# First MLP's second product on token blocks of 384 instead of 288

## The chip, the core and the metric

The kernel runs on one core of a Trainium2 chip. The metric is device time of one execution in microseconds (us). Before the change it is 1552.22 us, the median of three runs (1552.0 to 1557.69).

## What is computed

Two-step attention through 32 packed vectors per head, then two MLPs, all in float32 (8 batches, 8 heads, 576 tokens, so 4608 tokens of 512 features):

```python
p_packed = sm_attn(p, k, v)
out = sm_attn(q, p_packed, p_packed)
x = out.transpose(0, 2, 1, 3).reshape(4608, 512)
a = x @ w_a
b = x @ w_b
y = a * b @ w_out
h = y @ w_in
g = h * np.clip(h + 3.0, 0.0, 6.0) / 6.0
result = g @ w_out2
```

The change concerns `a * b @ w_out`, with d_ff = 1536.

## The kernel before, in words

A float32 product is made of three TensorE matmuls on values that are split into a high and a low part (`mm3`, lines 58 to 61: hi·hi on L59, lo·hi on L60, hi·lo on L61). Names ending in `_hi` and `_lo` are these parts.

**First stage.** Attention and the first MLP are interleaved. The outer loop has 48 steps `t`: four groups `g` of two batches (1152 tokens), and in each twelve blocks `m` of 128 hidden features. A step issues five units, in this order: `ab_unit(t, 0, 0)`, `pw_unit(t + 1)`, `ab_unit(t, 0, 1)`, `ab_unit(t, 1, 0)`, `ab_unit(t, 1, 1)`.

- `pw_unit` (L409 to L415) multiplies packed vectors and first-layer weights for the next step into two PSUM banks of the kind `att` (three exist); ScalarE makes `pw_hi` (L411), VectorE `pw_lo` (L415), which frees the banks.
- `ab_unit(t, b, h)` computes a and b of the hidden block for one half (288 tokens, `SH`) of one batch: 12 matmuls, 6 into each of two PSUM tiles, out of three `ab` banks. ScalarE copies a out (L435), VectorE multiplies by b (L437, `g`). Two ticks later `rest` makes `g_hi` on ScalarE (L443) and `g_lo` on GpSimd (L444). A tick is one unit or one `y_unit`.
- `y_unit(g, s, oc, r)` is the second product: for one block of 128 output features (`oc`, four of them), one token block `r` and three steps t (`SW` = 3), 9 matmuls into one of two `y` banks. The sum over the four `s` of a group is kept in SBUF (`acc`): copied by ScalarE for s = 0 (L462), added by VectorE after (L464), and stored to `y1d` at s = 3 (L466). Before, r counts four token blocks of 288, the same blocks that `ab_unit` makes.

So each three steps make 16 y units. They wait in a list, `y_ready`, and are put out one at a time at chosen places between the five units of a step. A y unit issued beside an `ab_unit` is what TensorE does while ScalarE and VectorE empty the `ab` banks.

Beside this, ScalarE, VectorE and GpSimd convert the weights from float64 (`piece_units`: `cv_` tiles and L81 to L96, results `rab`, `ro`, `p2f`), split `w_out` (`wo_split`, L392 and L393) and do the attention's softmax for the next batches (`s`, `et`, `pv`, `bd` are its products on TensorE). In most steps of the first group three pieces are converted (`w_a`, `w_b`, `w_out`), in the second and third group one piece for the second MLP, and two in every third step (t = 14, 17, up to 35). Each engine takes its instructions in the order in which the program issues them; the table of places in the step loop sets this order.

**Second stage.** The second MLP runs on tiles of 768 tokens, with products `h` (384 columns) and `o` (512 columns). The change does not touch it.

Of the kernel before, what the change touches and what calls it, by code (L numbers as in the profile page):

```python
# [8 lines left out]
F32 = mybir.dt.float32  # L9
F32R = mybir.dt.float32r  # L10
# [9 lines left out]
B, H, S, D, NP = 8, 8, 576, 64, 32  # L20
NT = B * S
DM, F1, F2 = 512, 1536, 2048
P = 128
NM1 = F1 // P
NM2 = F2 // P
SH = S // 2
NG = B // 2
TG = 2 * S
SW = 3
# [3 lines left out]
CP = 512  # L33
# [7 lines left out]
def f32(ap):  # L41
    return ap.bitcast(F32)
# [3 lines left out]
def tile_kernel(ctx: ExitStack, tc: tile.TileContext, qT, kT, vn, pT, wab, wo1, win, wo2, out):  # L46
# [9 lines left out]
    act, dve, pool, pe, sp = nc.scalar, nc.vector, nc.gpsimd, nc.tensor, nc.sync  # L56
# [46 lines left out]
    p2f = dram.tile([NM2, 2, P, CP], F32, name="p2f")  # L103
    y1d = dram.tile([DM // P, P, NT], F32, name="y1d")
# [7 lines left out]
    main = es_main.enter_context(tc.tile_pool(name="main", bufs=1))  # L112
    psum = es_main.enter_context(tc.tile_pool(name="psum", bufs=1, space=PSUM))
# [6 lines left out]
    def later(n, fn):  # L120
        due.append([n, fn])
# [232 lines left out]
    def piece_units():  # L354
        k = n_piece[1]
        n_piece[1] += 1
        m, i = pieces[k]
        if m >= NM1:
            o = att.tile([P, CP], F32, tag="p2f", name=f"p2f{m}_{i}", bufs=3)
            stores.append((p2f[m - NM1, i], o))  # L360
        elif i == 2:
            o = ro_tile(m)
            stores.append((wo1f[m * P:(m + 1) * P, :], o))
        else:
            if i == 0:
                rab_tile(m)
            o = rab_t[m][:, i * CP:(i + 1) * CP]
            stores.append((wabf[m][:, i * CP:(i + 1) * CP], o))

        def move():  # L370
            if k > 0 and k != n_first:
                sp.dma_start(*stores[k - 1])

        u = f64_round(att, raw64.pop(k), o, f"p{m}_{i}")
        last = u.pop()

        def end():
# [44 lines left out]
    def ab_unit(t, b, h):  # L422
        hi, lo = pw_t[t]
        ath, atl = at_t[2 * (t // NM1) + b]
        r = 2 * b + h
        ps = []
        for w in range(2):
            pt = psum.tile([P, 512], F32, tag="ab", name=f"ab{t}_{r}{w}", bufs=BANKS["ab"])[:, :SH]
            for c in range(2):
                ws = slice(w * P, (w + 1) * P)  # L430
                ts = slice(h * SH, (h + 1) * SH)
                mm3(pt, hi[:, c, b, ws], lo[:, c, b, ws], ath[:, c, ts], atl[:, c, ts], c == 0, c == 1)
            ps.append(pt)
        a = main.tile([P, SH], F32, tag="a", name=f"a{t}_{r}", bufs=2)
        act.copy(a, ps[0])  # L435
        g32 = main.tile([P, SH], F32, tag="g32", name=f"g32_{t}_{r}", bufs=3)
        dve.tensor_mul(g32, a, ps[1])  # L437
        gh = main.tile([P, SH], F32R, tag=f"g_hi{r}", name=f"g_hi{t}_{r}", bufs=SW + 1)
        gl = main.tile([P, SH], F32R, tag=f"g_lo{r}", name=f"g_lo{t}_{r}", bufs=SW + 1)
        g_t[t, r] = (gh, gl)  # L440

        def rest():
            act.copy(gh, g32)  # L443
            pool.tensor_sub(gl, g32, f32(gh))  # L444
            if t % SW == SW - 1:
                later(2, lambda: y_ready.extend((t // NM1, t % NM1 // SW, oc, r) for oc in range(DM // P)))

        later(2, rest)

    y_ready = []  # L450

    def y_unit(g, s, oc, r):
        ps = psum.tile([P, 512], F32, tag="y", name=f"y{g}_{s}{oc}{r}", bufs=BANKS["y"])[:, :SH]
        for i in range(SW):
            t = g * NM1 + s * SW + i
            gh, gl = g_t[t, r]
            oh, ol = wo_t[t, oc // 2]
            ws = slice(oc % 2 * P, (oc % 2 + 1) * P)
            mm3(ps, oh[:, ws], ol[:, ws], gh, gl, i == 0, i == SW - 1)
        if s == 0:  # L460
            acc_t[oc, r] = main.tile([P, SH], F32, tag=f"acc{oc}{r}", name=f"acc{g}_{oc}{r}", bufs=1)
            act.copy(acc_t[oc, r], ps)  # L462
        else:
            dve.tensor_add(acc_t[oc, r], ps, acc_t[oc, r])  # L464
        if s == NM1 // SW - 1:
            sp.dma_start(y1d[oc, :, g * TG + r * SH:g * TG + (r + 1) * SH], acc_t[oc, r])  # L466

# [212 lines left out]
    for t in range(NSTEP):  # L680
        g, m = divmod(t, NM1)
        if m == 0 and g + 1 < NG:
            lhs_tiles(g + 1)
            b = 2 * g + 2
# [28 lines left out]
        for i, (u, *x) in enumerate(units):  # L713
# [17 lines left out]
            for k in range(2):  # L731
                for _ in parts[2 * i + k]:
                    if not now:
                        now = piece_units()
                    now.pop(0)()
                for fn in todo[2 * i + k]:
                    fn()
                if y_ready and (k == 0 or i in (1, 3)) and (y_ready[0][0] * NM1 + y_ready[0][1] * SW + SW - 1, y_ready[0][2] // 2) in wo_t:
                    y_unit(*y_ready.pop(0))
                    tick()  # L740
    while due or y_ready:
# [193 lines left out]
```

## Time and profile before

| | us |
|---|---|
| median of three runs | 1552.22 |
| lowest, highest | 1552.0, 1557.69 |
| profiled execution, its own time | 1552.25 |
| profiled execution, its span | 1550.5 |
| TensorE matmul busy | 1491.7 (96% of the span) |
| weight loads busy | 1347.3 (87%) |
| VectorE busy | 872.3 (56%) |
| ScalarE busy | 682.0 (44%) |
| GpSimd busy | 491.9 (32%) |

A matmul's row shows a duration that reaches past the start of the next matmul, since they are pipelined; the distance between starts is the pace. Idle time in brackets at a row's end is that of the engine just before it, with what ended it. About 1.75 us of the execution lie outside the span.

### The profile page before, as it was taken

To read this page: it belongs to the slowest core of one execution; us is meant where nothing else is said; L and a number is where in the kernel's file an instruction comes from. 1 tells how busy PE (TensorE), PEld (TensorE's weight loads), DVE (VectorE), ACT (ScalarE), POOL (GpSimd) and SP (SyncE) were. 2 spreads that over 40 slices of the span, in tenths; PEclk is the share of its full clock that TensorE was granted. 3 is DMA by queue.
4 is the path that set the end of the run, shared out by engine and by line. 5 is a ranking of instruction groups with operands and counts; after the bars stand their busy time and mean duration, and the time that the engine had idled before them with its cause. 6 is when DMAs were issued, how large, how long until landed. Compare 5 with 4: busy or idle time off the path is not lost. (4 is left out here: it accounts for less than half of the span.)

```text
span 1550.5 us, 27991 instructions
## 1 busy us (share of the span) xinstructions
PE 1491.7 (96%) x11128; PEld 1347.3 (87%) x11128; DVE 872.3 (56%) x1592; ACT 682.0 (44%) x1453; POOL 491.9 (32%) x483
## 2 busy tenths in 40 slices
PE   4799999999999999999999999999999999999998
PEld 2588898888989899999989988998998998998997
DVE  5778784555754666545544464455455446455443
ACT  4566554554555545554423343343343334234332
POOL 2576653453634545554711130030020021011000
PEclk9799999999999999999999999999999999999999
DMA  8775555655466433664354334344344344333331
GB/s 288 218 220 177 184 191 176 194 160 179 124 198 188 138 125 106 235 219 170 120 180 178 129 141 178 116 162 149 130 152 167 107 172 143 136 144 133 142 138 41
DMA packets 75954, 250.06 MB, mean 161 GB/s; under 512 B 7856, under 2 KB 26288, under 8 KB 68784
## 3 DMA queue, kind: packets, MB, share of 16 engines
q1 hardware_dynamic: 75824, 248.28, 46.6%
q8 instruction: 87, 1.43, 0.4%
q14 instruction: 43, 0.35, 0.1%
HBM read 196.87 MB, written 51.38 MB: 160 GB/s over the span
## 5 line engine op out<-in xcount | busy, mean ns | idle before, releaser
L59 PE MATMUL ab<-at_hi,pw_hi 128*128 128x288 f32 x768 | 234.0, 305 | 8.3 <-ACT a L435 5.5
L61 PE MATMUL ab<-at_hi,pw_lo 128*128 128x288 f32 x768 | 229.1, 298 | 4.3 <-DVE pw_lo L415 4.3
L59 PE MATMUL y<-g_hi,wo_hi 128*128 128x288 f32 x768 | 231.3, 301 | 1.8 <-DVE acc L464 1.7
L60 PE MATMUL ab<-at_lo,pw_hi 128*128 128x288 f32 x768 | 228.6, 298 | 1.2 <-POOL at_lo L291 0.6
L61 PE MATMUL y<-g_hi,wo_lo 128*128 128x288 f32 x768 | 226.4, 295 | 1.0 <-POOL wo_lo L393 1.0
L60 PE MATMUL y<-g_lo,wo_hi 128*128 128x288 f32 x768 | 226.9, 295 | 0.4 <-POOL g_lo L444 0.4
L60 PE MATMUL o<-wo_lo,g2h 128*128 128x512 f32 x576 | 225.0, 391 | 0.0
L61 PE MATMUL o<-wo_hi,g2l 128*128 128x512 f32 x576 | 224.9, 390 | 0.0
L59 PE MATMUL o<-wo_hi,g2h 128*128 128x512 f32 x576 | 224.7, 390 | 0.0
L444 POOL TENSOR_TENSOR g_lo<-g,g_hi 128x288 fp32r<-128x288 f32 x192 | 164.4, 859 | 176.8 <-ACT g_hi L443 172.4
L783 DVE TENSOR_TENSOR g2l<-u,g2h 128x384 fp32r<-128x384 f32 x192 | 121.7, 634 | 140.9 <-ACT g2h L782 136.0
L437 DVE TENSOR_TENSOR g<-a,ab 128x288 f32<-128x288 f32 x192 | 86.4, 451 | 171.7 <-PE ab L61 112.3
L59 PEld LDWEIGHTS ab<-at_hi,pw_hi 128*128 128x128 f32 x768 | 146.6, 191 | 23.7 <-ACT a L435 7.6
L59 PEld LDWEIGHTS y<-g_hi,wo_hi 128*128 128x128 f32 x768 | 144.2, 188 | 19.4 <-DVE acc L464 9.1
L774 ACT ACTIVATE r<-c,half_b 128x384 f32<-128x384 f32 x144 | 88.9, 617 | 144.4 <-DVE c L767 143.9
L61 PEld LDWEIGHTS ab<-at_hi,pw_lo 128*128 128x128 f32 x768 | 146.3, 191 | 4.6 <-DVE pw_lo L415 4.5
L60 PEld LDWEIGHTS ab<-at_lo,pw_hi 128*128 128x128 f32 x768 | 146.5, 191 | 1.7 <-POOL at_lo L291 0.9
L570 POOL TENSOR_TENSOR ty_T<-raw_y 128x768 f32<-128x768 f32 x12 | 23.4, 1952 | 387.1 <-DMA raw_y<-y1d 387.1
L435 ACT COPY a<-ab 128x288 f32<-128x288 f32 x192 | 76.2, 400 | 157.9 <-PE ab L61 156.9
L61 PEld LDWEIGHTS y<-g_hi,wo_lo 128*128 128x128 f32 x768 | 144.3, 188 | 1.5 <-POOL wo_lo L393 1.5
L60 PEld LDWEIGHTS y<-g_lo,wo_hi 128*128 128x128 f32 x768 | 144.3, 188 | 0.6 <-POOL g_lo L444 0.6
L782 ACT CAST g2h<-u 128x384 fp32r<-128x384 f32 x192 | 98.7, 514 | 86.1 <-DVE u L776 84.7
(323 smaller groups left out, 3058.1 us busy)
## 6 DMA issues: line engine op xcount, KB each, us to landing
w<-w2d SPq DMA_DIRECT2D x47, 1792.0 KB, 7.3
rab<-wabf SPq DMA_DIRECT2D x36, 512.0 KB, 5.2
f64p<-in_wo SPq DMA_DIRECT2D x28, 512.0 KB, 3.7
w2d<-w SPq DMA_DIRECT2D x8, 1792.0 KB, 6.7
f64p<-in_wab SPq DMA_DIRECT2D x24, 512.0 KB, 4.6
k<-in_kT SPq DMA_DIRECT2D x16, 576.0 KB, 5.3
q<-in_qT SPq DMA_DIRECT2D x16, 576.0 KB, 5.2
ro<-wo1f SPq DMA_DIRECT2D x36, 256.0 KB, 3.7
```

Source lines behind the costliest of these rows:

```text
L59: pe.matmul(ps, lhsT=l_hi, rhs=r_hi, start=first, stop=False, skip_group_check=skip)
L60: pe.matmul(ps, lhsT=l_hi, rhs=r_lo, start=False, stop=False, skip_group_check=skip)
L61: pe.matmul(ps, lhsT=l_lo, rhs=r_hi, start=False, stop=last, skip_group_check=skip)
L435: act.copy(a, ps[0])
L437: dve.tensor_mul(g32, a, ps[1])
L444: pool.tensor_sub(gl, g32, f32(gh))
L570: pool.tensor_sub(z[to], get(a), get(b))
L774: act.activation(r, c, AF.Relu, bias=half_b, scale=1.0 / 6.0)
L782: act.copy(hi, u)
L783: dve.tensor_sub(lo, u, f32(hi))
```

## The change

The first product keeps its units of 288 tokens. The gated product of one batch is now one tile of 576 (`g32`), whose halves ScalarE and VectorE fill in place (the separate tile `a` is gone). When the second half is there, it is split into hi and lo parts by pieces that belong to three token blocks of 384 per group: 384 + 192 tokens of the first batch, 192 + 384 of the second (`PLACE`). The second product has three blocks r of 384, so 12 y units in three steps instead of 16. It is put out in at most five places of a step (before: seven). One conversion buffer (`p2f`) is given up: two in place of three.

```diff
+TY = 384
+
+PLACE = {0: [(0, TY, 0, 0), (TY, S, 1, 0)], 1: [(0, S - TY, 1, S - TY), (S - TY, S, 2, 0)]}
...
-            o = att.tile([P, CP], F32, tag="p2f", name=f"p2f{m}_{i}", bufs=3)
+            o = att.tile([P, CP], F32, tag="p2f", name=f"p2f{m}_{i}", bufs=2)
...
-        a = main.tile([P, SH], F32, tag="a", name=f"a{t}_{r}", bufs=2)
-        act.copy(a, ps[0])
-        g32 = main.tile([P, SH], F32, tag="g32", name=f"g32_{t}_{r}", bufs=3)
-        dve.tensor_mul(g32, a, ps[1])
-        gh = main.tile([P, SH], F32R, tag=f"g_hi{r}", name=f"g_hi{t}_{r}", bufs=SW + 1)
-        gl = main.tile([P, SH], F32R, tag=f"g_lo{r}", name=f"g_lo{t}_{r}", bufs=SW + 1)
-        g_t[t, r] = (gh, gl)
-
-        def rest():
-            act.copy(gh, g32)
-            pool.tensor_sub(gl, g32, f32(gh))
-            if t % SW == SW - 1:
+        if h == 0:
+            g32_t[0] = main.tile([P, S], F32, tag="g32", name=f"g32_{t}_{b}", bufs=3)
+        g32 = g32_t[0]
+        part = g32[:, h * SH:(h + 1) * SH]
+        act.copy(part, ps[0])
+        dve.tensor_mul(part, part, ps[1])
+        if h == 0:
+            return
+
+        def rest(t0, t1, r, r0):
+            n = t1 - t0
...
+            gh, gl = (x[:, r0:r0 + n] for x in g_t[t, r])
+            act.copy(gh, g32[:, t0:t1])
+            pool.tensor_sub(gl, g32[:, t0:t1], f32(gh))
+            if t % SW == SW - 1 and r0 + n == TY:
                 later(2, lambda: y_ready.extend((t // NM1, t % NM1 // SW, oc, r) for oc in range(DM // P)))
 
-        later(2, rest)
+        for i, x in enumerate(PLACE[b]):
+            later(2 + i, lambda x=x: rest(*x))
...
-        ps = psum.tile([P, 512], F32, tag="y", name=f"y{g}_{s}{oc}{r}", bufs=BANKS["y"])[:, :SH]
+        ps = psum.tile([P, 512], F32, tag="y", name=f"y{g}_{s}{oc}{r}", bufs=BANKS["y"])[:, :TY]
...
-                if y_ready and (k == 0 or i in (1, 3)) and (y_ready[0][0] * NM1 + y_ready[0][1] * SW + SW - 1, y_ready[0][2] // 2) in wo_t:
+                if y_ready and k == 0 and (y_ready[0][0] * NM1 + y_ready[0][1] * SW + SW - 1, y_ready[0][2] // 2) in wo_t:
```

How the order moves, in the step t = 14 (a third step of its three). First TensorE, before. `ab_10`, `ab_11` are the two PSUM tiles of `ab_unit(14, 0, 1)`, `ab_20` and `ab_30` those of the second batch's halves, the digits of `y_012` are s, oc and r. Of each unit the first row is shown:

```order
L59 MATMUL ab_30_3757<-at_hi_3231,pw_hi_3342 128x288
...
L59 MATMUL ab_00_3840<-at_hi_1739,pw_hi_3599 128x288
...
L409 MATMUL pw_0_3875<-rab_3364,lhs_697 32x256
...
L59 MATMUL ab_10_3915<-at_hi_1739,pw_hi_3599 128x288
...
L59 MATMUL ab_20_3945<-at_hi_3231,pw_hi_3599 128x288
...
L59 MATMUL y_000_3969<-g_hi_0_3318,wo_hi_3366 128x288
...
L59 MATMUL y_010_3983<-g_hi_0_3318,wo_hi_3366 128x288
...
L59 MATMUL ab_30_3995<-at_hi_3231,pw_hi_3599 128x288
...
L176 MATMUL s_400_4015<-q_3340,lhs_3297 32x288
...
L59 MATMUL y_020_4029<-g_hi_0_3318,wo_hi_3431 128x288
...
L176 MATMUL s_410_4043<-q_3340,lhs_3297 32x288
```

The same place now:

```order
L63 MATMUL ab_30_3425<-at_hi_2997,pw_hi_3069 128x288
...
L63 MATMUL y_312_3458<-g_hi_2_2689,wo_hi_2609 128x384
...
L63 MATMUL ab_00_3518<-at_hi_1648,pw_hi_3294 128x288
...
L63 MATMUL y_322_3545<-g_hi_2_2689,wo_hi_2650 128x384
...
L413 MATMUL pw_0_3564<-rab_3091,lhs_686 32x256
...
L63 MATMUL y_332_3594<-g_hi_2_2689,wo_hi_2650 128x384
...
L63 MATMUL ab_10_3616<-at_hi_1648,pw_hi_3294 128x288
...
L63 MATMUL ab_20_3640<-at_hi_2997,pw_hi_3294 128x288
...
L63 MATMUL ab_30_3663<-at_hi_2997,pw_hi_3294 128x288
...
L180 MATMUL s_400_3683<-q_3067,lhs_3023 32x288
...
L180 MATMUL s_410_3697<-q_3067,lhs_3023 32x288
...
L63 MATMUL ab_00_3711<-at_hi_1648,pw_hi_3562 128x288
```

Every y unit now has an `ab_unit` or the `pw_unit` on either side; in place of `ab_30`, `ab_00`, `pw`, `ab_10`, `ab_20` in a row, now the four units `ab_10`, `ab_20`, `ab_30`, `ab_00` follow each other without a y unit, which makes three bare successions in every three steps; and the attention's `s_400` and `s_410` have no y unit between them.

ScalarE in the same step, before:

```order
L411 CAST pw_hi_3873<-pw_0_3875 128x512
L411 CAST pw_hi_3873<-pw_1_3876 128x512
L443 CAST g_hi_0_3858<-g_14_0_3856 128x288
L392 CAST wo_hi_3899<-ro_3555 128x256
L81 ACTIVATE cv_sqp_1_3908<-f64p_1_3176 128x512
L82 ACTIVATE p2f_1_3907<-f64p_1_3176 128x512
L435 COPY a_1_3929<-ab_10_3915 128x288
L435 COPY a_2_3959<-ab_20_3945 128x288
L443 CAST g_hi_1_3933<-g_14_1_3931 128x288
```

And now:

```order
L415 CAST pw_hi_3562<-pw_0_3564 128x512
L415 CAST pw_hi_3562<-pw_1_3565 128x512
L396 CAST wo_hi_3586<-ro_3251 128x256
L85 ACTIVATE cv_sqp_1_3609<-f64p_1_2936 128x512
L86 ACTIVATE p2f_1_3608<-f64p_1_2936 128x512
L442 COPY g_14_0_3532<-ab_10_3616 128x288
L442 COPY g_14_1_3654<-ab_20_3640 128x288
L455 CAST g_hi_0_3657<-g_14_0_3532 128x384
L442 COPY g_14_1_3654<-ab_30_3663 128x288
```

One `g_hi` has left the stretch between `pw_hi` and the copy out of `ab_10`.

VectorE in the same step, before:

```order
L84 TENSOR_SCALAR cv_ap_1_3911<-f64p_1_3176 128x512
L437 TENSOR_TENSOR g_14_1_3931<-a_1_3929,ab_11_3922 128x288
L415 TENSOR_TENSOR pw_lo_3874<-pw_0_3875,pw_hi_3873 128x512
L415 TENSOR_TENSOR pw_lo_3874<-pw_1_3876,pw_hi_3873 128x512
L88 SCALAR_TENSOR_TENSOR cv_ap_1_3911<-f64p_1_3176,cv_ap_1_3911 128x512
```

And now:

```order
L477 TENSOR_TENSOR acc_32_1638<-y_332_3594,acc_32_1638 128x384
L419 TENSOR_TENSOR pw_lo_3563<-pw_0_3564,pw_hi_3562 128x512
L419 TENSOR_TENSOR pw_lo_3563<-pw_1_3565,pw_hi_3562 128x512
L88 TENSOR_SCALAR cv_ap_1_3612<-f64p_1_2936 128x512
L443 TENSOR_TENSOR g_14_0_3532<-g_14_0_3532,ab_11_3623 128x288
L92 SCALAR_TENSOR_TENSOR cv_ap_1_3612<-f64p_1_2936,cv_ap_1_3612 128x512
```

`pw_lo` now stands ahead of the multiplication that needs `ab_11`, and behind the addition that needs the y unit after `pw`.

## Rows read from the trace of the kernel before

**Rows 1.** Busy time of each engine in three stretches: start, both stages.

```profile
core 0: us, PE busy (x) PEld busy (x) DVE busy (x) ACT busy (x) POOL busy (x), PEclk, DMA share, GB/s
0.00:100.00 100.00, 66.83 (x828) 48.16 (x829) 69.22 (x133) 53.55 (x122) 46.40 (x46) 0.86 0.78 252
100.00:794.00 694.00, 678.86 (x6566) 627.00 (x6565) 420.08 (x799) 352.17 (x830) 358.07 (x387) 1.00 0.52 169
794.00:1550.00 756.00, 745.99 (x3739) 672.11 (x3737) 382.97 (x662) 276.31 (x501) 87.47 (x51) 1.00 0.39 143
```

**Rows 2.** TensorE's waits from 100 to 790 us: total, times, longest.

```profile
PE s L176 <- DVE pw_lo L415: 4.7, 4, 2.7
PE ab L59 <- ACT a L435: 4.2, 7, 0.7
PE pw L409 <- POOL rab L96: 2.3, 2, 1.8
PE y L59 <- DVE acc L464: 1.7, 2, 1.3
...
PE y L60 <- POOL g_lo L444: 0.4, 1, 0.4
...
PE y L61 <- POOL wo_lo L393: 0.3, 1, 0.3
```

**Rows 3.** Costliest groups of the page: the second product's matmuls.

```profile
L59 PE MATMUL y<-g_hi,wo_hi 128*128 128x288 f32 x768 | 231.3, 301 | 1.8 <-DVE acc L464 1.7
L61 PE MATMUL y<-g_hi,wo_lo 128*128 128x288 f32 x768 | 226.4, 295 | 1.0 <-POOL wo_lo L393 1.0
L60 PE MATMUL y<-g_lo,wo_hi 128*128 128x288 f32 x768 | 226.9, 295 | 0.4 <-POOL g_lo L444 0.4
```

**Rows 4.** Timeline of TensorE where the first stage ends: start, duration, what.

```profile
772.05 0.29 PE L59 MATMUL y<-g_hi,wo_hi 128*128 128x288 f32 x1
...
792.84 0.34 PE L59 MATMUL h_0x<-yh_B,w 128*128 128x384 f32 x1
...
795.79 0.34 PE L61 MATMUL h_0x<-yh_B,w 128*128 128x384 f32 x1
```

**Rows 5.** Timeline of TensorE in step 14, at its wait.

```profile
275.98 0.29 PE L60 MATMUL ab<-at_lo,pw_hi 128*128 128x288 f32 x1
276.11 0.29 PE L61 MATMUL ab<-at_hi,pw_lo 128*128 128x288 f32 x1
277.12 0.40 PE L59 MATMUL ab<-at_hi,pw_hi 128*128 128x288 f32 x1 [0.72 <-ACT a L435]
277.36 0.30 PE L60 MATMUL ab<-at_lo,pw_hi 128*128 128x288 f32 x1
```

**Rows 6.** Timeline of ScalarE in step 14, up to that wait.

```profile
273.95 1.07 ACT L411 CAST pw_hi<-pw 128x512 fp32r<-128x512 f32 x2
274.90 0.45 ACT L443 CAST g_hi<-g 128x288 fp32r<-128x288 f32 x1
275.24 0.42 ACT L392 CAST wo_hi<-ro 128x256 fp32r<-128x256 f32 x1
...
276.67 0.70 ACT L435 COPY a<-ab 128x288 f32<-128x288 f32 x2
```

**Rows 7.** Timeline of VectorE and TensorE in step 17, at the longest attention wait.

```profile
319.93 1.04 DVE L84 TENSOR_SCALAR cv_ap<-f64p 128x512 uint32<-128x512 uint32 x1
322.18 0.45 DVE L437 TENSOR_TENSOR g<-a,ab 128x288 f32<-128x288 f32 x1 [1.21 <-ACT a L435]
322.55 1.28 DVE L415 TENSOR_TENSOR pw_lo<-pw,pw_hi 128x512 fp32r<-128x512 f32 x2
...
323.38 0.71 PE L176 MATMUL s<-k,p 64*32 64x288 f32 x14 [2.69 <-DVE pw_lo L415]
```

**Rows 8.** Timeline of TensorE: neighbouring attention units, and the wait for converted weights.

```profile
66.22 0.73 PE L176 MATMUL s<-k,p 64*32 64x288 f32 x7 [2.54 <-ACT ex L189]
...
129.44 0.45 PE L409 MATMUL pw<-rab,lhs 64*32 64x256 f32 x8 [1.81 <-POOL rab L96]
```

**Rows 9.** Groups by line: sums and splits at 288, and copies at 384.

```profile
L464 DVE TENSOR_TENSOR acc<-y,acc 128x288 f32<-128x288 f32 x192 | 86.5, 452 | 78.7 <-PE y L61 78.0
L767 DVE TENSOR_TENSOR c<-u,h_5z 128x384 f32<-128x384 f32 x12 | 6.6, 552 | 0.1
L462 ACT COPY acc<-y 128x288 f32<-128x288 f32 x64 | 25.5, 401 | 51.1 <-PE y L61 50.8
L845 ACT COPY s<-h_2x 128x384 f32<-128x384 f32 x6 | 2.9, 479 | 17.8 <-PE h_2x L61 17.8
```

**Rows 10.** Timeline of the DMA queue and ScalarE: a `p2f` store, the second-next write.

```profile
455.74 0.40 SPq L372 DMA_DIRECT2D p2f<-p2f  x1
...
461.63 0.67 ACT L82 ACTIVATE p2f<-f64p 128x512 int32<-128x512 uint16 x1
```

**Rows 11.** Instructions on the tile `p2f` from 300 to 660 us: its DMAs.

```profile
DMA to landing us min/median/max: 2.0/3.7/8.7
```

More of the change, by code (lines that the diff above doesn't have):

```diff
@@ L433, in ab_unit @@
             ps.append(pt)
-        a = main.tile([P, SH], F32, tag="a", name=f"a{t}_{r}", bufs=2)
-        act.copy(a, ps[0])
-        g32 = main.tile([P, SH], F32, tag="g32", name=f"g32_{t}_{r}", bufs=3)
-        dve.tensor_mul(g32, a, ps[1])
-        gh = main.tile([P, SH], F32R, tag=f"g_hi{r}", name=f"g_hi{t}_{r}", bufs=SW + 1)
-        gl = main.tile([P, SH], F32R, tag=f"g_lo{r}", name=f"g_lo{t}_{r}", bufs=SW + 1)
-        g_t[t, r] = (gh, gl)
-        def rest():
-            act.copy(gh, g32)
-            pool.tensor_sub(gl, g32, f32(gh))
-            if t % SW == SW - 1:
+        if h == 0:
[8 more added lines that the diff above has]
+            n = t1 - t0
+            if r0 == 0:
+                g_t[t, r] = (
+                    main.tile([P, TY], F32R, tag=f"g_hi{r}", name=f"g_hi{t}_{r}", bufs=SW + 1),
+                    main.tile([P, TY], F32R, tag=f"g_lo{r}", name=f"g_lo{t}_{r}", bufs=SW + 1),
+                )
+            gh, gl = (x[:, r0:r0 + n] for x in g_t[t, r])
+            act.copy(gh, g32[:, t0:t1])
+            pool.tensor_sub(gl, g32[:, t0:t1], f32(gh))
+            if t % SW == SW - 1 and r0 + n == TY:
                 later(2, lambda: y_ready.extend((t // NM1, t % NM1 // SW, oc, r) for oc in range(DM // P)))
-        later(2, rest)
-    y_ready = []
+        for i, x in enumerate(PLACE[b]):
+            later(2 + i, lambda x=x: rest(*x))
+    y_ready, g32_t = [], {}
     def y_unit(g, s, oc, r):
-        ps = psum.tile([P, 512], F32, tag="y", name=f"y{g}_{s}{oc}{r}", bufs=BANKS["y"])[:, :SH]
+        ps = psum.tile([P, 512], F32, tag="y", name=f"y{g}_{s}{oc}{r}", bufs=BANKS["y"])[:, :TY]
         for i in range(SW):
@@ L460, in y_unit @@
         if s == 0:
-            acc_t[oc, r] = main.tile([P, SH], F32, tag=f"acc{oc}{r}", name=f"acc{g}_{oc}{r}", bufs=1)
+            acc_t[oc, r] = main.tile([P, TY], F32, tag=f"acc{oc}{r}", name=f"acc{g}_{oc}{r}", bufs=1)
             act.copy(acc_t[oc, r], ps)
@@ L465, in y_unit @@
         if s == NM1 // SW - 1:
-            sp.dma_start(y1d[oc, :, g * TG + r * SH:g * TG + (r + 1) * SH], acc_t[oc, r])
+            sp.dma_start(y1d[oc, :, g * TG + r * TY:g * TG + (r + 1) * TY], acc_t[oc, r])
     PROD = {1: (0, "B11"), 2: (1, "B21"), 3: (6, "B22"), 4: (2, "T4"), 5: (3, "T1"), 6: (4, "T2"), 7: (5, "T3")}
```

## The prediction

> **What bounds the kernel now.** I read the busy times by stretch first. From 100 us on TensorE is busy for 679 of 694 us in the first stage and for 746 of 756 in the second, with a granted clock of 1.00 (the 2.4 GHz level) in both [rows 1]. Only the first 100 us, with 67 us busy, are bound by something else. So the time is the number of matmuls times their pace, plus what TensorE waits; the other engines (VectorE 420 of 694 us in the first stage) count only where TensorE waits for them. The second view, TensorE's waits, lists these for the first stage: 4.7 us of attention products for `pw_lo`, 4.2 of `ab` units for ScalarE's copy, 2.3 of `pw` for converted weights, and 2.4 of y units for three releasers [rows 2]. The third, the page's groups, counts what the change regroups: 3 x 768 = 2304 matmuls of 288 columns [rows 3]. Their durations (295 to 301 ns) are not what one costs, since matmuls overlap; the cost is the distance between starts, from the timeline.
>
> **Part 1: fewer, wider matmuls.** Between the y unit at 772.05 and the first `h` at 792.84 lie 16 y units and one `ab` unit, 144 + 12 = 156 matmuls of 288 columns without a wait: 20.79 us / 156 = 133.3 ns. From there the second stage's `h` has 384 columns, the size that y gets: 17 starts in 2.95 us, 173.5 ns [rows 4]. The y products cost 2304 x 133.3 ns = 307.1 us, and would cost 1728 x 173.5 ns = 299.8 us. All of it lies on TensorE's path: **7.3 us less**. At 2.4 GHz 288 columns are 120.0 ns and 384 are 160.0, so each matmul pays some 13 ns beside its columns, and 576 fewer pay it.
>
> The Trainium skill states another price for that fixed part: its page "TensorE: Matmul & The Clock Gate", section "Back-to-back issue gap", gives N / 2.4 + 2.5 ns when warm, so 122.5 and 162.5 ns here. By it the term would be an estimated 2304 x 122.5 - 1728 x 162.5 ns, 1.4 us in place of 7.3. The row is of this program's own stream, with a weight load before each matmul, and it decides.
>
> **Part 2: the waits that the new order touches.** What a wait costs is more than its idle time. At 277.12 the row says 0.72 idle, but the starts lie 1.01 us apart, 0.88 more than the pace, and the next one follows after 0.24 rather than 0.13: 0.99 in all, the idle time plus 0.27 [rows 5].
>
> *`ab` units for the copy.* Seven waits, 4.2 us [rows 2], 4.2 + 7 x 0.27 = 6.1 us. The one in step 14 comes from ScalarE's queue behind `pw_hi`: 1.07 us of `pw_hi`, then `g_hi`, `wo_hi` and a conversion, and the copy out of `ab_10` starts only at 276.67 [rows 6]. The new order puts a y unit, 9 x 173.5 ns = 1.56 us, between `pw` and `ab_10`, and one `g_hi` (0.34 us to the next start) leaves the queue ahead of the copy. That is 1.9 us against 0.88 late. Bounds: 0 and 6.1 us of gain; I take **6.1**.
>
> *y units for their bank, `g_lo`, `wo_lo`.* 2.4 us in four waits [rows 2], with 4 x 0.27 some 3.5 us. Two y units no longer stand side by side, so a y bank has at least one `ab` unit (12 x 133.3 ns = 1.60 us) or a `pw` unit more to be emptied in, and `g_lo` is asked for half a step later. Bounds 0 and 3.5; I take **3.5**.
>
> *Attention products for `pw_lo`.* The longest is 2.69 us: `pw_lo` stood behind a multiplication that waited 1.21 us for ScalarE's late copy [rows 7]. It now stands ahead of that multiplication. Bounds 0 and 4.7 + 4 x 0.27 = 5.8; the others of the four keep their neighbours, so I take **2.0**.
>
> *New: four `ab` units in a row.* There are three bare successions in each of 16 groups of three steps, 48 in all. VectorE empties the second bank of each unit (0.45 us) and has `pw_lo` (1.28 us) and conversions in the same stretch [rows 7]; its queue decides whether the third and fourth unit wait. Bounds: no loss, or 0.99 us [rows 5] at each of the 48, 47.5 us. The row nearest to it is the kernel's own chain before, where only seven such waits appear in 16 groups. I take 0.4 us at each of the 11 third steps with two or three conversions: **4.4 us lost**.
>
> *New: attention units side by side.* In steps 2 and 14 two `s` units follow each other without work between; they need four banks of three. Between nothing and 2.54 us each, the wait of such a pair in the start [rows 8]; I take **2.0 us lost** for both, below the upper end, since the banks are asked to be emptied while TensorE's queue is otherwise ahead of VectorE by little.
>
> *Early steps.* At 129.44 `pw` waits 1.81 us for converted weights [rows 8], which TensorE's pace does not hasten. Ahead of it stand 16 y units (19.2 us) before and 11 (17.2 us) now; if the weights come when they came, the twelfth, 1.56 us, is left over, and the pace gain of the first two groups of 16 (2 x 0.46) goes into the wait. Bounds 0 and 2.5; I take **2.5 us lost**.
>
> **What lies beside TensorE's path.** VectorE's sums into `acc` go from 192 x 452 ns = 86.8 us to 144 x 552 = 79.5, ScalarE's copies from 64 x 401 ns = 25.7 to 48 x 479 = 23.0 [rows 9]. The splits keep their number (192) and their columns, 384 + 192 in place of 288 + 288. All this is hidden under TensorE, costed at nothing. So are the 16 stores fewer on the DMA queue. ScalarE's copy, and no longer VectorE, now waits where `g32` is still being read, but three whole tiles give that five units of distance. The last group ends with 12 y units after the last `ab` in place of 14; their sum is in part 1. If that cover is gone, what shows is ScalarE's queue, at most rows 5's loss each time.
>
> **The lost conversion buffer.** A piece may now overwrite `p2f` only when the store of the second piece before it has landed. In the closest pair the store is issued at 455.74 and the write comes at 461.63 [rows 10]; with the median landing of 3.7 us 2.2 us remain, with the longest, 8.7 us, ScalarE would stand for 2.8 us [rows 11]. Costed at 0, with 2.8 as the upper end.
>
> **Sum.** -7.3 - 6.1 - 3.5 - 2.0 + 4.4 + 2.0 + 2.5 = -10.0 us. Against the profiled execution's own 1552.25 us (span 1550.5; the median of the three runs is 1552.22, the same within 0.03) that is **1542.2 us**, 0.64% less. A measurement of this kernel can tell about 0.5%, 7.8 us, from no change: below 1544.5 is faster, above 1560.0 slower.
>
> **Rivals.** *All old waits go and none comes*: 7.3 + 6.1 + 3.5 + 2.0 = 18.9 us, 1533.4. For it: ScalarE and VectorE are about half busy in the first stage. Against it: the bare chain and the `s` pairs are new.
>
> *The pace alone*: waits move and their sum stays, 1552.25 - 7.3 = 1544.9 us, just within no change. For it: a chain of bare units exists before and after, in the same third steps.
>
> *Cost goes by columns*: a matmul pays in proportion to its columns, 384 / 288 x 133.3 = 177.7 ns, and 1728 of them cost 307.1 us as before. Then only the waits are left, -2.7 us, 1549.5. Against it: 173.5 ns at 384 columns [rows 4]. The Trainium skill's rule of part 1 points to this side, with 1.4 us.
>
> *Slower: the bare chain binds.* In each third step VectorE's queue (the multiplications behind `pw_lo` and conversions) releases the `ab` banks too late, and two of three successions wait as in rows 5: 32 x 0.99 = 31.7 us. With the pace and the old `ab` waits gone, 1552.25 - 7.3 - 6.1 + 31.7 = 1570.6 us. It decides from 22 such waits on, since the other terms sum to -14.4 and 7.8 have to be lost beyond. For it: VectorE is the next busiest engine, and the first group converts three pieces in a step. Against it: the seven waits of `ab` before were for ScalarE's copy [rows 2], and the one read stood behind `pw_hi` [rows 6], which now lies ahead of a y unit.
>
> That the change does not do what it says is excluded by the instructions: 576 matmuls are gone.
>
> **Chances and range.** Forecast 0.60, its own range 1537 to 1547 (0.52 of it below 1544.5); all waits go 0.15; pace alone 0.17 (0.04 of it below 1544.5); by columns 0.03; slower 0.05. So faster 0.52 + 0.15 + 0.04 = 0.71, same 0.08 + 0.13 + 0.03 = 0.24, slower 0.05. The range 1534 to 1549 takes in the pace alone, most of the case without waits and the ends of the smaller terms, and leaves out the binding chain.
>
> **What would show it.** In the profile after: 3 x 576 y matmuls of 384 columns at a pace near 173.5 ns; the wait of `ab` for the copy down from 4.2 us to under 1, or, if I am wrong, a larger one for VectorE's multiplication in third steps; y's wait for `acc` gone; `s` in step 17 not waiting 2.7 us, but new short waits in steps 2 and 14; a longer wait of `pw` for `rab` near 129 us. The second stage should keep its 756 us. A y pace of 177 ns, or ScalarE waiting for DMA at `p2f`, would make the forecast wrong.

## The result and the profile after

The changed kernel takes 1563.86 us (median of four runs, 1562.85 to 1567.7), the kernel before 1552.37 beside it: a ratio of 1.006, 95% interval [1.004, 1.008]. The forecast was 1542.2 us, a gain of 10.0; the profiled executions differ by a loss of 10.6 (1562.85 against 1552.25). The matmuls became cheaper as forecast; two losses that the prediction did not look at, and one that it priced too low, ate that and as much again.

Busy time in stretches of the changed kernel, columns as in [rows 1]:

```profile
0.00:100.00 100.00, 61.76 (x793) 42.22 (x794) 69.03 (x131) 51.17 (x117) 44.19 (x44) 0.88 0.77 252
100.00:800.00 700.00, 681.29 (x6024) 623.87 (x6023) 420.02 (x751) 343.53 (x820) 364.88 (x389) 1.00 0.50 167
800.00:1560.50 760.50, 745.88 (x3739) 672.27 (x3737) 382.56 (x662) 276.31 (x501) 88.08 (x51) 1.00 0.39 142
```

TensorE is 5 us less busy in the first 100 us and stands idle for some 19 us from 100 to 800, against 15 before. What it waits for there (answers to [rows 2]; all line numbers are 4 higher up to the first stage's loop):

```profile
PE ab L63 <- ACT g L442: 8.8, 12, 1.7
PE pw L413 <- POOL rab L100: 3.8, 2, 3.6
PE pv L230 <- ACT et L219: 2.4, 2, 1.2
PE s L180 <- DVE t L258: 1.9, 2, 1.7
PE s L180 <- DVE pw_lo L419: 1.5, 2, 0.7
```

The y units wait for nothing there now and the attention less for `pw_lo` (1.5 for 4.7 us), both as forecast. But the `ab` units wait for ScalarE's copy twice as long, 8.8 for 4.2 us, and `pv`, an attention product, waits 2.4 us for ScalarE's `et` (0.6 before). The pace is in the timeline of TensorE at the end of the first stage (answers to [rows 4]):

```profile
795.79 0.33 PE L63 MATMUL y<-g_hi,wo_hi 128*128 128x384 f32 x1
...
798.92 0.33 PE L63 MATMUL h_0x<-yh_B,w 128*128 128x384 f32 x1
```

18 starts in 3.13 us, 173.9 ns; and there are 1728 of them, in three groups like this one (the page's costliest groups, answer to [rows 3]):

```profile
L63 PE MATMUL y<-g_hi,wo_hi 128*128 128x384 f32 x576 | 198.7, 345 | 0.0
```

**Where the time went.** I compare the starts of the same unit in the two traces. The first `h` comes at 798.92 for 792.84 [rows 4], 6.1 us late; the last matmul starts at 1555.39 for 1545.39, so the second stage, which the change does not touch, takes 756.5 for 752.6 us. The last 0.6 us lie behind it. In the first stage, the `pw` unit for step 12 ("step 12" below) comes 6.9 us later although the matmuls put out until there (35 y units for 48) are 432 x 133.3 - 315 x 173.5 ns = 2.9 us cheaper: some 9.9 us are lost in the start and the first group, to waits and to the lower clock behind them. At the first `h` it is 6.1 + 7.3 = 13.4.

**Theory A: a buffer of `g_hi`.** The waits of ScalarE from 100 to 800 us hold a row, the first here, that the kernel before does not have:

```profile
ACT g_hi L455 <- PE y L65: 54.7, 15, 4.5
ACT g_hi L455 <- DVE g L443: 24.6, 27, 2.1
```

These 15 waits stand one in each group of three steps, in the third step. ScalarE's timeline in step 35 shows what one does, and TensorE's what comes of it:

```profile
605.81 0.51 ACT L455 CAST g_hi<-g 128x384 fp32r<-128x384 f32 x1 [3.64 <-PE y L65]
...
607.36 1.05 ACT L415 CAST pw_hi<-pw 128x512 fp32r<-128x512 f32 x2
608.30 0.41 ACT L396 CAST wo_hi<-ro 128x256 fp32r<-128x256 f32 x1
...
609.75 0.68 ACT L442 COPY g<-ab 128x288 f32<-128x288 f32 x2
```

```profile
610.18 0.40 PE L63 MATMUL ab<-at_hi,pw_hi 128*128 128x288 f32 x1 [0.96 <-ACT g L442]
```

`g_hi` of token block 2 has four buffers (`SW` + 1). In step 35 ScalarE makes block 2 of step 34, in the buffer that held step 30, and step 30 is read by the y units of steps 30 to 32. The last of these now stands right behind `pw`; its first three matmuls, the ones that read the old buffer, end ScalarE's wait. So ScalarE stands 3.64 us, and behind it in its queue two conversions, `pw_hi`, `wo_hi` and the copy out of `ab` come late. The order of ScalarE shown above for step 14 begins at `pw_hi`; the `g_hi` that waits stands just ahead of it. Before, y units had up to seven places in a step and began within the third step already; the wait was not there.

**Theory B: the first group.** There the order puts out y units later than before, and TensorE runs dry where conversions bind. TensorE's timeline at two places:

```profile
93.12 1.21 PE L180 MATMUL s<-q,lhs 64*32 64x288 f32 x14 [3.84 <-DVE t L258]
...
148.33 1.93 PE L413 MATMUL pw<-rab,lhs 64*32 64x256 f32 x24 [3.63 <-POOL rab L100]
...
151.00 0.52 PE L65 MATMUL y<-g_hi,wo_lo 128*128 128x384 f32 x1
151.32 0.52 PE L63 MATMUL y<-g_hi,wo_hi 128*128 128x384 f32 x1
```

The first is the second of two neighbouring `s` units of step 2. The second is a wait for converted weights, but not the one of [rows 8]: that one, 1.81 us in `pw` for step 6, has shrunk to 0.17 us (at 130.18), and this one stands in `pw` for step 7, which the kernel before reaches at 146.40 without a wait. A third, 1.75 us of an `s` unit for `t`, follows in step 8 (196.26).

After the wait at 148.33 the y matmuls start 320 ns apart, which is 384 columns at 1.2 GHz, the lower level of the clock, for some 3 us. The kernel before has such a stretch behind its own wait at 129.44, where 288 columns take 240 ns. The granted clock (the third number from the end) in the changed kernel, then in the one before:

```profile
148.00:160.00 12.00, 11.67 (x76) 10.41 (x77) 7.29 (x14) 5.26 (x12) 5.42 (x6) 0.74 0.51 168
```

```profile
130.00:133.00 3.00, 3.00 (x28) 2.59 (x16) 1.91 (x3) 2.44 (x5) 1.28 (x3) 0.64 0.90 280
```

**Theory C** is the lost conversion buffer, **theory D** the second stage: there TensorE waits longer for ScalarE's first copy of a tile.

```profile
PE h_1x L63 <- ACT s L858: 5.1, 6, 2.6
PE h_1x L63 <- DMA w<-w2d: 1.4, 1, 1.4
```

Before, the first of these is 2.3 us in 6 places, and the second is not there. ScalarE's timeline at the fourth of the six tiles, after and then before (lines 13 apart):

```profile
1191.21 0.59 ACT L812 COPY os<-o 128x512 f32<-128x512 f32 x1 [5.46 <-DMA out<-os]
```

```profile
1180.71 0.59 ACT L799 COPY os<-o 128x512 f32<-128x512 f32 x1 [2.91 <-DMA out<-os]
```

Three output buffers `os` serve six rows of stores at a change of tiles, so the fourth copy waits for a store. There the first three stores land 4.6 to 4.9 us after issue, before 2.0 to 2.5.

### The profile page after: what moved, and what is told of

Read it like the earlier page. It is cut to its first block, busy times and chain, and to the rows that moved or that the text cites. A ratio compares the mean times of both kernels' runs of the same rounds, so it can differ in the third digit from the quotient of the medians.

```text
span 1560.9 us, 26687 instructions
## 1 busy us (share of the span) xinstructions
PE 1488.9 (95%) x10552; PEld 1338.4 (86%) x10552; DVE 871.6 (56%) x1544; ACT 671.0 (43%) x1437; POOL 497.1 (32%) x483
## 4 chain that ended last, share of the span: by engine, by line
PE 80%; DVE 5%; ACT 5%; DMA 3%; POOL 3%; issue 2%; SPq 0%; ACTq 0%; DVEq 0%; POOLq 0%
PE o L64 8%; PE o L65 8%; PE o L63 8%; PE y L63 6%; PE y L65 6%; PE y L64 6%; PE ab L63 5%; PE ab L65 5%; PE ab L64 5%; PE pw L413 3%; DMA out<-os 1%; PE s L180 1%; DMA raw_y<-y1d 1%; ACT cv_sqp L85 1%; POOL g_lo L456 1%
## 5 line engine op out<-in xcount | busy, mean ns | idle before, releaser
L456 POOL TENSOR_TENSOR g_lo<-g,g_hi 128x384 fp32r<-128x384 f32 (+1 forms) x192 | 166.4, 873 | 177.6 <-ACT g_hi L455 170.3
L63 PE MATMUL y<-g_hi,wo_hi 128*128 128x384 f32 x576 | 198.7, 345 | 0.0
L65 PE MATMUL y<-g_hi,wo_lo 128*128 128x384 f32 x576 | 194.7, 338 | 0.0
L64 PE MATMUL y<-g_lo,wo_hi 128*128 128x384 f32 x576 | 194.2, 337 | 0.0
L443 DVE TENSOR_TENSOR g<-g,ab 128x288 f32<-128x288 f32 x192 | 85.7, 448 | 122.9 <-PE ab L65 86.6
L442 ACT COPY g<-ab 128x288 f32<-128x288 f32 x192 | 76.5, 401 | 162.4 <-PE ab L65 159.5
L477 DVE TENSOR_TENSOR acc<-y,acc 128x384 f32<-128x384 f32 x144 | 79.9, 555 | 105.8 <-PE y L65 105.2
L65 PEld LDWEIGHTS o<-wo_hi,g2l 128*128 128x128 f32 x576 | 108.1, 188 | 23.1
L63 PEld LDWEIGHTS y<-g_hi,wo_hi 128*128 128x128 f32 x576 | 108.5, 188 | 19.0 <-issue 9.1
```

The lines of the kernel that those rows point to most:

```text
L63: pe.matmul(ps, lhsT=l_hi, rhs=r_hi, start=first, stop=False, skip_group_check=skip)
L64: pe.matmul(ps, lhsT=l_hi, rhs=r_lo, start=False, stop=False, skip_group_check=skip)
L65: pe.matmul(ps, lhsT=l_lo, rhs=r_hi, start=False, stop=last, skip_group_check=skip)
L442: act.copy(part, ps[0])
L443: dve.tensor_mul(part, part, ps[1])
L456: pool.tensor_sub(gl, g32[:, t0:t1], f32(gh))
```

## The experiments

Ratios, with 95% intervals, are against the kernel before, which was run again beside each (medians of 1552.9 to 1555.8 us); they and not the times are to be compared. "First `h`" and "step 12" are of one profiled execution against the one of the kernel before. Two executions can lie some 4 us apart there (see the conversion buffer), so smaller differences than that do not show an edit's effect by themselves.

**The late piece.** The second piece of the second batch (block 2) is split three places later, after the y units that read the old buffer.

```diff
-            later(2 + i, lambda x=x: rest(*x))
+            later(5 if b == 1 and i == 1 else 2 + i, lambda x=x: rest(*x))
```

> The changed kernel, but the last piece of the second batch (the 384 tokens that go to block r = 2) is split three ticks later, so that its g_hi stands on ScalarE behind pw_hi and the conversions and no longer ahead of them while it waits for the last y unit to give its buffer free. Theory A (ScalarE stands at that g_hi, 3.6 us in step 35, and everything behind it is late): the ab units' wait for ScalarE's copy falls from 8.8 us (12 waits) to under 2, and the time from 1563.9 to 1552 to 1557. Theory B (the loss is made in the first group, where y units now start later and TensorE has less to do while converted weights are awaited): the ab waits fall, but the 3.8, 3.6 and 1.7 us waits before 200 us stay, 1558 to 1562. Theory C (two buffers of p2f in place of three): nothing changes, 1562 to 1565.

Measured: 1553.18 us, ratio 0.9997 [0.9981, 1.0014]. ScalarE's wait for y fell from 54.7 us to 1.6, TensorE's wait for its copy from 235 us on from 7.6 us to 0.7; first `h` -7.1 us in place of +6.1 (step 12: +3.9 for +6.9). The early waits stayed (`s` for `t` 4.3 us, `pw` for `rab` 3.4), and so did the second stage's loss (758.2 us). That is 13 us in the first stage; it does not yet say whether it is the buffer or the move of a copy.

**Sooner y units.** The y units of the first group are asked for one place sooner, then those of all groups.

```diff
-                later(2, lambda: y_ready.extend(
+                later(1 if t < NM1 else 2, lambda: y_ready.extend(
```

> The changed kernel, but in the first group alone y units become ready one tick sooner, so that the first one of each three steps stands between the attention units s_200 and s_210 (or ahead of the last ab unit's successor) again and all follow one place earlier. Theory A: ab waits after 235 us stay, and the time falls by less than 3, to 1561 to 1563, by the waits of the first group alone. Theory B: the waits of 3.8 us at 93 and of 3.6 at 148 go, pw of step 12 comes 5 to 8 us sooner, 1556 to 1559. Theory C: 1562 to 1565.

Measured: 1559.41 us, 1.0029 [1.0015, 1.0042]. The waits for `t` and `rab` in the first group fell to 0.9 and 0.2 us, step 12 from +6.9 to +2.0 us; TensorE's wait for the copy from 235 us on, 8.0 us, stayed. The interval still touches that of the changed kernel ([1.004, 1.008]).

```diff
+                later(1, lambda: y_ready.extend(
```

> The changed kernel, y units ready one tick sooner in all groups. The last y unit then stands ahead of pw, so the g_hi that waits for it is released about 2 us sooner, but pw and the next ab unit stand side by side again. Theory A: most of ScalarE's standing goes everywhere, 1552 to 1558; Theory B: the first group's loss goes, 1556 to 1559, ab waits stay near 8 us. A and B together: 1548 to 1554. Theory C: 1562 to 1565.

Measured: 1563.71 us, 1.0068 [1.0045, 1.0091]. Asked for sooner in all groups, y loses: it then waits for `g_lo` on GpSimd (7.0 us in 6 places from 235 us on), first `h` +4.3. So the place that the change chose is right for `g_lo`, and wrong for the buffer.

**The conversion buffer alone**, in the kernel before.

```diff
-            o = att.tile([P, CP], F32, tag="p2f", name=f"p2f{m}_{i}", bufs=3)
+            o = att.tile([P, CP], F32, tag="p2f", name=f"p2f{m}_{i}", bufs=2)
```

> The kernel before with one edit of the change alone: two p2f buffers in place of three. Theories A and B: the same as before, 1551 to 1554. Theory C: most of the loss, 1558 to 1564, with ScalarE waiting for stores.

Measured: 1557.08 us, 1.0007 [0.9992, 1.0022]. Theory C is out as the cause of 10 us; up to 3.4 us are not excluded. ScalarE waits for no store of `p2f` in this trace, nor in the changed kernel's. Yet first `h` is at +4.2 us: at 135.18 `s` waits 2.28 us for `pw_lo` (0.77 before), and the granted clock is 0.50, the lower level, from 135 to 141 us (before: 131 to 134), and again from 325.8 to 329, behind a wait of 2.69 us that left it at 1.00 in the profile of the kernel before. This is how far two executions lie apart without a store in the way.

**Late piece and first group sooner** in one kernel (both diffs):

> The late second piece (the run that gave 0.9997 of the kernel before) and the earlier units of the first group (1.0029) in one kernel. Theory: two separate losses. One is ScalarE's wait for the last unit of the second product at each third step after 235 us (late piece: from +6 us at step 12 to -6 at step 45); the other is the first group's later units (earlier request: step 12 at +2 in place of +6.9). If they are separate, the sum holds: step 12 at about +1 or less against the kernel before, first unit of the second stage about 8 to 10 us ahead of it, and with the second stage's 4 to 6 us lost the time is 0.5 to 3 us lower than that of the late piece alone, near 1550. Rival: both act on the same early wait of ScalarE; then step 12 stays at +2 to +4 and the time equals that of the late piece alone within 1 us.

Measured: 1552.43 us, 0.9985 [0.9972, 0.9997]. Step 12 at +3.4 us, first `h` -7.1: as with the late piece alone (+3.9 at step 12, not the +6 that the expectation gives it), so the rival fits the first stage. y waits for `g_lo` (2.4 and 1.0 us) took the place of the old waits. What the first group gains by it is not seen at the first `h`.

**Four output buffers**, in that kernel, in the changed one and in the one before.

```diff
-                o = p2b.tile([P, DM], F32, tag="o", name=f"os{tt}_{n}", bufs=3)
+                o = p2b.tile([P, DM], F32, tag="o", name=f"os{tt}_{n}", bufs=4)
```

> As the run beside it, with four buffers in place of three for the output rows of the second stage. Theory D: the second stage loses its 4 to 6 us because the first output stores at a change of tiles land 4 to 5 us after issue in place of 2 to 2.5, and the fourth output's copy on ScalarE waits for the first store, with the next tile's first copies queued behind it. Then a fourth buffer takes away most of TensorE's wait for ScalarE's copy of the first product (5 to 7 us in the changed kernels, 2.3 before): it falls to 1 to 2.5 us, and the second stage from 756 to 758 us to 753 us or less; the time is 3 to 5 us lower than the run beside it. Rival: the second stage's loss lies elsewhere (the order of VectorE's copies, a clock step, missing matmul records); then this wait and the stage stay as they are within 1 us.

Measured: 1547.58 us, 0.9959 [0.9946, 0.9973]; the wait for ScalarE's copy from 6.9 to 3.6 us, the second stage from 759.7 to 754.4.

> The changed kernel with four buffers in place of three for the output rows of the second stage, and nothing else. Theory D: the second stage goes from 756.5 to about 753 us or less, the wait for ScalarE's copy of the first product from 5.1 to 1 to 2.5 us, the time from 1563.9 to about 1560. The first stage stays as in the changed kernel: first unit of the second stage 6 us later than in the kernel before. Rival (the loss lies elsewhere): 756 us again, time within 1 us of 1563.9.

Measured: 1560.02 us, 1.0041 [1.0025, 1.0057]; the wait from 5.1 to 1.4 us, the second stage from 756.5 to 752.2.

> The kernel before with four buffers in place of three for the output rows of the second stage. There the first stores land 2.0 to 2.5 us after issue, and the wait for ScalarE's copy of the first product sums to 2.3 us in 6 places. Theory D gives a gain of 0 to 2 us here, less than in the changed kernel; if the fourth buffer gains as much here as there (3 to 5 us), slower landing is not what sets the two kernels' second stages apart. Rival (loss elsewhere): no change within 1 us in both.

Measured: 1550.25 us, 0.998 [0.9968, 0.9993]; the wait from 2.3 to 0.5 us, the second stage from 752.6 to 749.6. The fourth buffer gains 3.0 us here and 4.2 there: it is where the loss shows, but of the 3.9 us between the two kernels it takes away only a third. Something still makes stores land late: with four buffers the stores at the same tile land after 2.5 to 4.2 us in the changed kernel.

**The packets of instructions.** The DMA view of 10 us around that change of tiles, first of the kernel before, then of the changed one (queue and kind, packets, MB, share; the stores' last number is the median us to landing):

```profile
q14 instruction: 1, 0.01, 0.2%
...
out<-os SPq DMA_DIRECT2D x6, 256.0 KB, 2.4
```

```profile
q8 instruction: 1, 0.02, 1.2%
...
out<-os SPq DMA_DIRECT2D x6, 256.0 KB, 3.6
```

Queue 8 carries packets of 16,384 bytes, of kind "instruction": 87 in the kernel before with 11,128 matmul records, 83 after with 10,552. That is 128 matmuls with their weight loads to a packet. The change removes 576 matmuls, 4.5 packets, so in the second stage every packet comes half a period elsewhere. In the changed kernel one starts 388.7 us after the first `h` and takes 1.9 us, right behind the first three stores (issued at 387.6 to 388.5); in the kernel before the nearest behind them is at 399.4. To test it, 32 small float32 products that nobody reads (64 matmul records, half a packet) at the start of each kernel:

```diff
+    pad = psum.tile([P, 512], F32, tag="att", name="pad", bufs=BANKS["att"])
+    for i in range(32):
+        q = i % 4
+        pe.matmul(pad[NP * q:NP * q + NP, :64], lhsT=ident[:, NP * q:NP * q + NP], rhs=ident[:, :64], start=True, stop=True)
```

> The changed kernel with 32 small float32 products (64 matmul records) of the identity at the start of the program, whose result nobody reads; nothing else. Theory of the instruction packets: queue 8 brings TensorE's instructions, one packet of 16,384 bytes to 128 matmuls with their weight loads; the change has 576 matmuls fewer, 4.5 packets, so in the second stage each packet falls half a period elsewhere, in the changed kernel onto the output stores at a change of tiles (388.7 us after the stage's first unit, stores issued at 387.6 to 388.5 and landed 4.5 to 4.9 us later), in the kernel before not (399.4). 64 more move the packets back: then the stores there land after 2 to 2.5 us again, the wait for ScalarE's copy of the first product falls from 5.1 to about 2.3 us, and the second stage from 756.5 us to 753 to 754 us. The first stage may be up to 2 us later for the added products. Rival (the packets only stand beside the slow stores): stage at 756 to 757 us, wait at 5 us.

> The kernel before with the same 32 small products at its start. Theory of the instruction packets: now they fall on the stores of this kernel: landing 4 to 5 us at one or two changes of tiles in place of 2.0 to 2.5, wait for ScalarE's copy of the first product 4 to 6 us in place of 2.3, second stage 755 to 757 us in place of 752.6. Rival (the slow stores belong to the changed kernel's buffers or work): second stage 752 to 753 us, as before.

Measured: 1561.81 us, 1.0048 [1.0031, 1.0064], for the changed kernel; 1561.27 us, 1.0047 [1.0028, 1.0067], for the kernel before. The second stage, first `h` to last matmul:

| | without | with the small products |
|---|---|---|
| kernel before | 752.6 | 756.4 |
| changed kernel | 756.5 | 752.1 |

They change places. The DMA view and the wait for ScalarE's copy, of the changed kernel with the small products (no row of queue 8 there):

```profile
out<-os SPq DMA_DIRECT2D x6, 256.0 KB, 2.2
```

```profile
PE h_1x L63 <- ACT s L863: 1.9, 6, 0.8
```

and of the kernel before with them:

```profile
q8 instruction: 1, 0.02, 0.7%
...
out<-os SPq DMA_DIRECT2D x6, 256.0 KB, 3.1
```

```profile
PE h_1x L59 <- ACT s L850: 5.3, 6, 2.1
```

So the second stage's 3.9 us come from where TensorE's instruction packets fall, and not from the change's buffers or work. All 16 traces agree: each ends six tiles in stores, 96 times in all, and 22 times a packet of queue 8 starts while the first three of these stores are under way. The slowest of the three then lands after 3.6 to 4.9 us, and after 3.0 at most the 74 other times. Nor is it a shift in time alone: the run with two `p2f` buffers reaches the first `h` 4.2 us later and keeps 752.7 us, the late piece reaches it 7.1 us sooner and has 758.2.

In total the products gained little or nothing: the changed kernel stays within its interval and the kernel before loses, since the first `h` comes 2.7 and 4.8 us later with them. How much of that they cost is not shown; it is within what two executions differ by.

**All three repairs**: late piece, first group sooner, four output buffers, and the small products.

> The run with the late second piece, the earlier first group and four output buffers (1547.6 us, second stage 754.4 us), with the same 32 small products at its start. Theory of the instruction packets: second stage 750 to 752.5 us, near the 749.6 us of the kernel before with four output buffers; time 1544 to 1547 us. Rival: 754 us again, time as without the small products or up to 2 us more.

Measured: 1542.7 us, 0.9921 [0.9905, 0.9936], second stage 751.0 us.

**A fifth buffer**, the direct test of A: no instruction moves.

```diff
-            g32_t[0] = main.tile([P, S], F32, tag="g32", name=f"g32_{t}_{b}", bufs=3)
+            g32_t[0] = main.tile([P, S], F32, tag="g32", name=f"g32_{t}_{b}", bufs=2)
...
-                    main.tile([P, TY], F32R, tag=f"g_hi{r}", name=f"g_hi{t}_{r}", bufs=SW + 1),
-                    main.tile([P, TY], F32R, tag=f"g_lo{r}", name=f"g_lo{t}_{r}", bufs=SW + 1),
+                    main.tile([P, TY], F32R, tag=f"g_hi{r}", name=f"g_hi{t}_{r}", bufs=SW + 1 + (r == 2)),
+                    main.tile([P, TY], F32R, tag=f"g_lo{r}", name=f"g_lo{t}_{r}", bufs=SW + 1 + (r == 2)),
```

> The changed kernel with a fifth buffer for the gated product's high and low parts of the second batch's first block (block 2), paid for with two in place of three buffers of the float32 product; no instruction is moved. Theory: ScalarE's wait at that block's copy for the last unit of the second product (54.7 us in 15 places from 100 to 800 us in the changed kernel, none with the late piece) is a wait for its buffer. Then it falls below 10 us, TensorE's wait of the first product for ScalarE's copy from 235 us on goes from about 8 us to under 2 us, and the first unit of the second stage comes 4 to 10 us sooner than in the changed kernel (+6 against the kernel before: -4 to +2). The first group stays as in the changed kernel (step 12 near +7). Rival: the late piece gained because a copy of ScalarE moved into an emptier step; then the fifth buffer leaves TensorE's wait at 7 us or more, and the first unit of the second stage within 2 us of the changed kernel's. A second rival from the cut float32 buffer: VectorE's product waits for GpSimd, and the gain is eaten.

Measured: 1551.62 us, 0.9972 [0.9958, 0.9987]. ScalarE's wait for y is gone from its list, and TensorE's waits from 235 to 790 us are down to this:

```profile
PE s L180 <- DVE pw_lo L419: 1.6, 2, 0.9
PE pw L413 <- ACT ex L193: 0.8, 1, 0.8
...
PE ab L63 <- ACT g L442: 0.2, 1, 0.2
```

The ratio falls from 1.006 to 0.9972. First `h` -9.6 us (step 12: +4.1), 15.7 us sooner than in the changed kernel and beyond what was expected; `pv` no longer waits for `et` either. Theory A is shown: no instruction moved, so the late piece did not gain by an emptier step. The smaller number of `g32` buffers now makes ScalarE wait for GpSimd (21.9 us in 10 places), without harm to TensorE. The second stage is at 758.6 us.

**The fifth buffer with the other repairs**, the small products placed where TensorE waits anyway (before the transpose of the second batch, at about 32 us); in the second run the first group sooner too.

```diff
             ps = bank(f"bd{b}")
+            for i in range(32 if b == 1 else 0):
+                q = i % 4
+                pe.matmul(ps[NP * q:NP * q + NP, 256:320], lhsT=ident[:, NP * q:NP * q + NP], rhs=ident[:, :64], start=True, stop=True)
```

> The run with the fifth buffer of block 2, with four output buffers and with 32 small products of the identity in an idle place of TensorE at about 32 us, to move the instruction packets. Theory: the three causes are separate. First stage as with the fifth buffer (first unit of the second stage 9.6 us ahead of the kernel before), second stage 750 to 751 us as in the run with all repairs (751.0): span some 1539, time 1540 to 1543 us. Rival (they overlap, or the small products cost what they give): 1546 us or more.

> The run beside it with the first group's units of the second product asked for one place sooner. Theory: the 4 us still lost at step 12 come from the later units; sooner takes away TensorE's waits for VectorE's t (3.8 us at 93 us) and GpSimd's rab (2.8 us), step 12 comes at +1 to +2 in place of +4, and the time is 1 to 3 us lower than the run beside it. Rival: waits for GpSimd's low part (2.4 and 1.0 us in the earlier run with both) take their place, step 12 stays at +3 to +4 and the time within 1 us.

Measured: 1540.02 us, 0.9911 [0.9895, 0.9928], and 1538.7 us, 0.9897 [0.9878, 0.9916]. First `h` -9.5 and -9.4, second stage 749.9 and 749.6: the three gains add. The run with sooner units stands 1 us better at step 12 (+2.7 for +3.7), but at step 27 both stand at -2.7: in both an `s` unit waits 1.8 us for `pw_lo` between (at 423.05 and 424.54), and behind it the granted clock is 0.50 from 423.7 to 427 in this run and 1.00 in the other. The last one is the fastest kernel of the study, 1.0% below the kernel before; its interval overlaps with that of the one beside it. The busy time of the first of the two, columns as above:

```profile
100.00:785.00 685.00, 677.00 (x6027) 624.39 (x6026) 417.79 (x751) 346.10 (x822) 361.25 (x389) 1.00 0.51 171
785.00:1538.00 753.00, 744.21 (x3736) 671.89 (x3734) 382.37 (x662) 276.12 (x501) 87.94 (x51) 1.00 0.39 143
```

From 100 us on TensorE stands 8 us in the first stage in place of 19.

## Why the prediction was wrong

| step of the sum | forecast | measured |
|---|---|---|
| fewer, wider matmuls | -7.3 | 173.9 ns for 173.5: -6.6 |
| `ab` units for the copy | -6.1 | 12 waits for 7, 4.6 us more; at the prediction's price 12.0 us for 6.1, so +5.9 |
| y units | -3.5 | gone |
| attention for `pw_lo` | -2.0 | 3.2 us less idle |
| four `ab` units in a row | +4.4 | no wait for VectorE's multiplication after 110 us |
| neighbouring `s` units | +2.0 | 3.84 us in step 2, 0.2 in step 14, and 1.75 in step 8 |
| early steps | +2.5 | the wait for `rab` near 129 us gone but for 0.17, 3.63 in the next `pw` unit; a stretch at the lower clock behind it, as before behind the other |
| `pv` for ScalarE's `et` | no term | 2.4 us for 0.6 |
| second stage | 0 | +3.9 |

**The pace was right.** The rule of the Trainium skill weighed there, its page "TensorE: Matmul & The Clock Gate", section "Back-to-back issue gap", would give an estimated 162.5 ns. The Trainium skill's page states it for one matmul by itself and not for a stream of weight loads and matmuls like this one, which the prediction does not say; the trace has 173.9 ns, so the measurement decides.

**The step that failed first** is "*`ab` units for the copy* ... I take 6.1". It looked at one `g_hi` that leaves ScalarE's queue, and at the order of what is left; it did not ask when each of these instructions may start. The text gives that look to `g32` ("three whole tiles give that five units of distance") and not to `g_hi` and `g_lo`, whose four buffers did not grow while their readers, the y units, were put later. Its own sentence "`g_lo` is asked for half a step later" names the delay that makes the buffer late and books it as a gain. What the runs showed in its place: ScalarE stands for that buffer 54.7 us in 15 places, and a fifth buffer takes 15.7 us off the first stage. It then comes to -9.6 us, where the forecast's terms sum to -10.0, but that is partly luck: the four `ab` units in a row cost nothing from 110 us on where 4.4 us were booked, and at step 12 that kernel still has lost some 7.0 us (4.1 + 2.9 of cheaper matmuls) where 3.5 were booked.

**The rival "the bare chain binds"** had the sign and the place, third steps, but its releaser was wrong: it was ScalarE's copy, not VectorE's multiplication. The 12 waits stay under the 22 from which it was to decide; what made the result slower was their sum with the early steps and the second stage.

**The early terms were too small.** The start and the first group lost some 9.9 us, not 3.5 (2.5 for the early steps and 1.0 for the neighbours in step 2); with the fifth buffer it is some 7.0, so up to 3 of it may be A's. The wait for converted weights did not grow where it was expected, near 129 us, but came one `pw` unit later. Why those weights come later than before was not found. Both neighbouring units and late y units count there, and an earlier request takes some of the waits away. But that is worth little by the end: the kernels with five buffers stand at +4.1, +3.7 and +2.7 us at step 12 and at -9.6, -9.5 and -9.4 at the first `h`. Between the last two it is the lower clock between steps 24 and 27; 1 us is in any case less than two executions differ by.

**"The second stage should keep its 756 us"** (the stretch of [rows 1], 752.6 us between first `h` and last matmul) failed for a reason that no row on this stage's work holds: 576 matmuls fewer ahead of it moved the instruction packets onto its stores, 3.9 us.

**The lost conversion buffer**, costed at 0, held in the changed kernel. [rows 11] counts loads of `p2f` too: its stores alone land after 3.1 us in the median and 8.4 at most, which leaves the term as it was. In five of the later runs ScalarE does wait once for such a store, for 0.8 to 1.7 us, and in two more for 0.2.

## What to carry to other kernels

When readers are put later, count the buffers of what they read: the writer of the next round waits, and everything behind it in its queue does too. A change that alters the number of matmuls ahead of an untouched stage can move that stage by some us through the instruction packets; half a packet of small products at an idle place tells it apart from a real cost, and a buffer more behind the stores makes it cheap. Two faults in a good change can hide it: repair one at a time before giving it up.

## What the runs showed of the hardware

A packet of instructions that falls among stores makes them land late: the slowest of the first three after 3.6 to 4.9 us, in 22 places of 16 traces, and after 3.0 at most without one. The page's DMA section gives both queues as shares of the same 16 engines, and the packet at 388.7 took 1.9 us beside the 4.9 us that the slowest store there took; that the store waits for the part of it that shares the packet's engine fits this and was not tested by itself. The Trainium skill's page "Runtime: NRT & Kernel Launch", section "Instruction fetch mechanics", describes a refill in blocks of 16 KiB, or 256 instructions, through the sequencer's own DMA queue. This agrees with the 128 matmuls and 128 weight loads to a packet here. The Trainium skill's page calls the cost of a block boundary mostly hidden; the crossed runs show 3.8 and 4.4 us in one stage, not in TensorE's supply of instructions but in the stores beside it.

After the wait of 3.63 us at 148.33 TensorE ran its matmuls at the lower clock: the granted clock was 0.74 in the mean of 148 to 160 us, between the levels of 1.2 and 2.4 GHz, and y starts were 320 ns apart at first. The sum had priced such a wait at its idle time plus 0.27 us; this one cost 9 x (320 - 173.9) ns = 1.3 us more. The kernel before pays a like price behind its wait of 1.81 us at 129.44. A like wait does not always bring it: of the two last runs, with the same wait of 1.8 us, one went on at a granted clock of 0.50 and one at 1.00.
